# Attention and a squared-ReLU MLP on one core: softmaxes with row maximum, casting loads and a shared set of PSUM banks

## The chip, the cores and the metric

The kernel runs on one core of one Trainium2 chip. The metric is the device time of an execution in microseconds (us), median of the runs shown. The traces come from the hardware profiler. Engines: PE multiplies matrices (PEld loads its weights), DVE works on vectors, ACT evaluates activations, POOL is a slower general engine, SP only issues DMAs here. ACT and POOL can issue DMAs too.

## What is computed

For each of 8 batches and 8 heads, 32 packing queries p attend to 576 keys and values, and the 32 packed rows are then both keys and values for the 576 queries q. The result, laid out as 4608 tokens of 512, goes through an MLP with a squared ReLU. All inputs and outputs are float32.

```python
def sm_attn(qq, kk, vv):
    s = scale * np.matmul(qq, kk.transpose(0, 1, 3, 2))
    s = s - np.max(s, axis=-1, keepdims=True)
    a = np.exp(s)
    a = a / (np.sum(a, axis=-1, keepdims=True) + 1e-09)
    return np.matmul(a, vv)
p_packed = sm_attn(p, k, v)
out = sm_attn(q, p_packed, p_packed)
...
h = x @ w_in
r = np.maximum(h, 0.0)
return ((r * r) @ w_out).astype(np.float32)
```

## The kernel before

Everything on PE is in bfloat16. The work goes batch by batch (b = 0 to 7), the eight heads as two quads (qd = 0, 1) of four heads, whose 4 x 32 packed rows fill 128 partitions or columns. The steps carry names that both texts use:

- **Loads.** SP issues every load of k, q, v (lines 404 and 411) and of the weights (434, 443) as float32 into staging tiles, and also the stores of the output (651, four for each 128 tokens). Only the first load of p comes from ACT. After the load a cast to bfloat16 is made: for batch 0 by ACT, DVE or POOL, for the others on POOL (line 351, or 349 on ACT), the weights on POOL or DVE.
- **Tk, Tq, X.** DVE transposes k (468) and q (462) in 32 x 32 blocks. X spreads the transposed p into a block matrix `pT_bd`, on POOL from batch 1 on.
- **S1.** Scores of p against k, with the 576 keys on the partitions (478, and 492 for the last 64), then an exponential without any maximum (485, 499).
- **PV.** The weights times v, in PSUM already transposed (513), and the denominators by matmuls with a column of ones (517). XT copies the packed rows out of PSUM as `pq_bd` (DVE and ACT, `pq_block`) and `ppT` (`extract`), with the reciprocal `rD` of the denominators.
- **M.** Since the second attention only mixes 32 packed rows per head, w_in is folded into them: M = ppT times w_in, 8 small matmuls for each of 4 chunks of 512 columns (548). It is copied out with the scale rD, one quad on ACT (556) and one mostly on DVE (558).
- **S2 and N.** Scores of q against the packed rows, packed rows on the partitions (578), exponential with scale rD (585), sums over the 32 rows by a matmul with a block matrix of ones (590), then logarithm, exponential of its negative (595, 600) and a multiply on DVE (606) give the weights `a2`.
- **F1.** For 16 blocks of 128 hidden columns: four matmuls of 288 columns (618), ReLU on ACT (626; on DVE, 628, for three blocks of batch 0) and the square on DVE (633) into `gT`, which holds two batches.
- **F2.** For 36 tiles of 128 tokens: 16 matmuls of 512 columns against w_out (642), a copy out of PSUM (349 or 351) and the stores.

PSUM has three pools: `a` of two banks (S1, PV, M), `h` of two double banks (F1, S2, N) and `o` of two banks (F2).

The order of the work on every engine is fixed when the program is made. `Plan` simulates all steps with given durations and lists them by earliest time; streams are listed by priority (attention ahead of F1, F1 ahead of F2), and a step may name other steps that it follows, slots of buffers that it takes, and slots that it frees. Engines then work through their own lists in order. S1 of batch b comes in the plan after F1 of batch b-2.

Of the kernel before, what the change touches and what calls it, by code (L numbers as in the profile page):

```python
# [10 lines left out]
ALU = mybir.AluOpType  # L11
F32 = mybir.dt.float32
BF16 = mybir.dt.bfloat16

P = 128
D = 64
NP = 32
QH = 4
# [19 lines left out]
class Step:  # L38
# [4 lines left out]
    def __init__(self, name, segs, deps=(), take=(), give=(), lag=0.0):  # L43
        self.name, self.deps, self.take, self.give, self.lag = name, list(deps), list(take), list(give), lag
        self.pieces = [[Piece(self, i, k, p) for k, p in enumerate(st)] for i, st in enumerate(segs)]
        self.give_at = [[(p, t or name) for p, j, t in self.give if j == i] for i in range(len(segs))]


class Plan:
# [3 lines left out]
    def __init__(self, slots):  # L53
        self.nslots = slots
        self.streams, self.base = [], {}
        self.fill = 0
# [4 lines left out]
    def forward(self):  # L61
# [4 lines left out]
        held, done, out = {}, {}, []  # L66
        pos = [0] * len(self.streams)
# [3 lines left out]
        def ready(st, t):  # L71
# [7 lines left out]
            for p, n in st.take:  # L79
# [8 lines left out]
                t = max(t, last[p])  # L88
            return t, pred

# [34 lines left out]
        while True:  # L125
            best = None
            for i, (prio, steps) in enumerate(self.streams):
# [7 lines left out]
                if key is None:  # L135
                    key = greedy(pc, t) + 0.003 * prio
                if t < INF and (best is None or key < best[0]):
                    best = (key, pc, t, pred, i)
            for x in pend:
                key = x[0].late  # L140
                if key is None:
                    key = greedy(x[0], x[1]) + 0.003 * (x[2] - 0.5)
# [4 lines left out]
            _, pc, t, pred, src = best  # L147
            b = None
# [11 lines left out]
            if pc.stage == 0:  # L160
                pos[src] += 1
                since[src] = s
                prio = self.streams[src][0]
                for p, k in st.take:
# [15 lines left out]
            for p, taker in st.give_at[i]:  # L180
                x = (fin + lag, tuple((q, lag) for q in ends))
                for j in held.pop((p, taker)):
                    slots[p][j] = x
            if i + 1 < len(st.pieces):
# [8 lines left out]
            s[pos[i]].name for i, (_, s) in enumerate(self.streams) if pos[i] < len(s)]  # L193
        return out, max(p.end for p in out)
# [39 lines left out]
    def first(self, rounds):  # L234
        best = None
        for r in range(rounds + 1):
            out, T = self.forward()
            v = self.score(out, T)
            if best is None or v < best[0]:
                best = (v, T, [(p, p.start, p.end, p.alt) for p in out])  # L240
# [9 lines left out]
    def vary(self, best, seed):  # L250
# [15 lines left out]
        return self.score(out, T), T, [(p, p.start, p.end, p.alt) for p in out]  # L266

    def run(self, rounds=0, seeds=()):
# [4 lines left out]
        self.log = []  # L273
        free = dict(self.base)
# [13 lines left out]
def kernel_impl(tc, q, k, v, p, w_in, w_out, out):  # L288
# [7 lines left out]
    NCB = DMODEL // P  # L296
    NWC = DFF // WCH
    HALF = S // 2
    JH = JT // 2
    TOK = B * S  # L300
    NW = 6
    NT = TOK // P

    with ExitStack() as ctx:
        ctx.enter_context(tc.manual_schedule())
        consts = ctx.enter_context(tc.tile_pool(name="consts", bufs=1))
        stg = ctx.enter_context(tc.tile_pool(name="stg", bufs=4))
        qkv = ctx.enter_context(tc.tile_pool(name="qkv", bufs=4))
        vpool = ctx.enter_context(tc.tile_pool(name="vpool", bufs=1))
# [5 lines left out]
        ps_att = ctx.enter_context(tc.tile_pool(name="ps_att", bufs=2, space=bass.MemoryType.PSUM))  # L315
        ps_h = ctx.enter_context(tc.tile_pool(name="ps_h", bufs=2, space=bass.MemoryType.PSUM))
        ps_o = ctx.enter_context(tc.tile_pool(name="ps_o", bufs=2, space=bass.MemoryType.PSUM))
# [5 lines left out]
        ones_bd = consts.tile([P, P], BF16, name="ones_bd")  # L323
        ones_c = consts.tile([P, 33], BF16, name="ones_c")
        msk = consts.tile([P, 32], BF16, name="msk")
        kT = consts.tile([P, NQD, (GM + 1) * P], F32, name="kT")
        idle_b = consts.tile([P, 256], BF16, name="idle_b")
        v_f = consts.tile([P, H, (GM + 1) * D], F32, name="v_f")
        pT = consts.tile([P, B * NQD, 32], F32, name="pT")
        pT_bd = [consts.tile([P, 896], BF16, name=f"pT_bd{i}") for i in range(2)]  # L330
        pq_bd = [consts.tile([P, 896], BF16, name=f"pq_bd{i}") for i in range(2)]

# [20 lines left out]
        def setup():  # L353
            nc.vector.memset(v_f[:, :, GM * D:], 0.0)
            nc.vector.memset(pT_bd[0][:, :BDW + 2 * P], 0.0)
            nc.vector.memset(ones_c[:, :1], 8.0)
            nc.vector.memset(msk, 0.0)
            nc.vector.memset(msk[:].rearrange("p (x y) -> p x y", y=4)[:, :, :2], 8.0)
# [541 lines left out]
```

## Time and profile before

| | |
|---|---|
| median of 3 runs | 272.71 us (270.44 to 276.31) |
| profiled execution, its span on the core | 272.6 us |
| PE busy | 245.0 us, 1840 matmuls |
| DVE, ACT, POOL busy | 169.6, 167.8, 80.1 us |
| HBM read, written | 37.22 MB, 9.44 MB |
| mean granted PE clock | 0.980 |

The profile has one execution. Its page gives the busy time of the engines and, in 40 slices of the span, the busy share in tenths (9 is 90% or more) of each engine and of the 16 DMA engines. Matmuls are pipelined, so the duration of one is longer than its spacing from the next; the spacing is what a full PE pays. A group of instructions is given by line, engine, operation, output<-inputs, shapes and count, then busy time, mean duration in ns and the idle time before it with its cause. The chain in order of time is followed back from the last instruction, at each step to what released it: start, duration, what.

### The profile page before, as it was taken

The numbers are of one execution on the slowest core, as the hardware profiler recorded it, in microseconds if no ns is written. First come the engines' busy times: TensorE is split into PE (matmuls) and PEld (weight loads), VectorE is DVE, ScalarE is ACT, GpSimd is POOL, SyncE is SP. The second block draws the span as 40 slices with busy tenths as digits, with TensorE's granted clock in tenths as the row PEclk, the third lists the DMA queues.
The fourth block names the chain that finished last, engine by engine and source line by source line (L and its number), as shares of the span: only waits on it lengthen the run. The fifth ranks groups of instructions, "written<-read, shape, count | busy, mean of one in ns | idle before, by whom it ended". The sixth has DMA issues, their size and how long they took to land.

```text
span 272.6 us, 5046 instructions
## 1 busy us (share of the span) xinstructions
PE 245.0 (90%) x1840; PEld 136.5 (50%) x1840; DVE 169.6 (62%) x327; ACT 167.8 (62%) x298; POOL 80.1 (29%) x99
## 2 busy tenths in 40 slices
PE   0558859999998889989999999999999999999993
PEld 0522533555664345745655665566446646644441
DVE  4658997999798498599687648963354504510000
ACT  3547735966786857778659776877657816831110
POOL 5242595592594831443170403000000000000000
PEclk9999995999999979999999999999999999999999
DMA  7999999965949994149328412110211122112222
GB/s 257 321 377 396 383 386 394 358 214 159 319 164 287 364 356 151 42 135 368 95 63 248 182 31 59 41 36 22 62 41 39 39 59 59 40 42 76 77 77 77
DMA packets 26744, 46.99 MB, mean 172 GB/s; under 512 B 5728, under 2 KB 13920, under 8 KB 26720
## 3 DMA queue, kind: packets, MB, share of 16 engines
q1 hardware_dynamic: 26192, 46.55, 51.6%
q8 instruction: 14, 0.23, 0.4%
q10 hardware_dynamic: 528, 0.13, 0.2%
q14 instruction: 10, 0.08, 0.1%
HBM read 37.22 MB, written 9.44 MB: 171 GB/s over the span
## 4 chain that ended last, share of the span: by engine, by line
PE 52%; DMA 18%; DVE 15%; SPq 5%; POOL 3%; issue 3%; ACT 2%; POOLq 0%; DVEq 0%
PE ps_o L642 29%; PE ps_h L618 15%; DVE gT L633 6%; DMA out_dram<-o_sb 5%; DMA w_f<-in_moe_w_in_dram 5%; DMA kq_f<-in_q_dram 5%; DMA v_f<-in_v_dram 4%; PE ps_a L548 3%; SPq L651 3%; DVE kT L468 3%; DVE M L558 2%; SPq L411 2%; PE ps_s L578 2%; ACT o_sb L349 1%; POOL v_b L351 1%
## 5 line engine op out<-in xcount | busy, mean ns | idle before, releaser
L642 PE MATMUL ps_o<-w_out_b,gT 128*128 128x512 bf16 x576 | 150.5, 383 | 0.5 <-DVE gT L633 0.4
L626 ACT ACTIVATE r<-ps_h 128x576 bf16<-128x576 f32 x125 | 79.4, 652 | 24.2 <-PE ps_h L618 18.1
L633 DVE TENSOR_TENSOR gT<-r 128x576 bf16<-128x576 bf16 x128 | 70.5, 573 | 36.5 <-ACT r L626 35.5
L618 PE MATMUL ps_h<-a,M 128*128 128x288 bf16 x512 | 84.1, 294 | 4.4 <-DVE r L628 3.3
L642 PEld LDWEIGHTS <-gT 128*128 128x128 bf16 x576 | 55.2, 98 | 51.6 <-issue 6.0
L618 PEld LDWEIGHTS <-M 128*128 128x128 bf16 x512 | 50.3, 100 | 33.8 <-issue 7.7
L349 ACT COPY o_sb<-ps_o 128x512 f32<-128x512 f32 x27 | 15.8, 585 | 35.0 <-DMA out_dram<-o_sb 23.0
L556 ACT ACTIVATE M<-ps_a,rD 128x512 bf16<-128x512 f32 x36 | 24.2, 689 | 8.6 <-PE ps_a L548 8.5
L351 POOL CAST q_b<-kq_f 128x1152 bf16<-128x1152 f32 (+1 forms) x16 | 19.0, 1203 | 29.3 <-DVE M L558 12.0
L558 DVE TENSOR_SCALAR M<-ps_a,rD 128x512 bf16<-128x512 f32 x28 | 20.7, 746 | 8.8 <-PE ps_a L548 8.6
L351 POOL CAST v_b<-v_f 128x1280 bf16<-128x1280 f32 (+1 forms) x15 | 18.8, 1280 | 21.1 <-PE ps_pp L517 10.2
L462 DVE STREAM_TRANSPOSE qT<-q_b 128x1152 bf16<-128x1152 bf16 x16 | 21.3, 1358 | 4.0 <-POOL q_b L351 3.9
L548 PE MATMUL ps_a<-w_in_b,ppT 64*32 64x512 bf16 x256 | 17.5, 434 | 4.2 <-DVE M L558 2.8
L468 DVE STREAM_TRANSPOSE kT<-k_b 128x320 f32<-128x320 f32 (+1 forms) x32 | 18.9, 686 | 2.8 <-PE ps_a L492 2.3
L351 POOL CAST k_b<-kq_f 128x1152 bf16<-128x1152 f32 (+1 forms) x15 | 18.1, 1210 | 7.6 <-DMA kq_f<-in_k_dram 6.6
L478 PE MATMUL ps_a<-pT_bd,kT 128*128 128x128 bf16 x128 | 9.6, 230 | 9.4 <-DVE pT_bd L351 8.0
L585 ACT ACTIVATE e<-ps_s,rD 128x576 bf16<-128x576 f32 x16 | 11.3, 739 | 9.4 <-PE ps_s L578 6.8
L351 POOL COPY pT_bd<-pT 32x128 bf16<-32x128 bf16 x28 | 10.3, 369 | 21.4 <-PE ps_a L492 15.0
L606 DVE TENSOR_TENSOR a<-e,rs 128x576 bf16<-128x576 bf16 x16 | 14.2, 890 | 0.0
L478 PEld LDWEIGHTS <-kT 128*128 128x128 bf16 x128 | 8.4, 103 | 11.5 <-DVE kT L468 9.1
L578 PE MATMUL ps_s<-qT,pq_bd 128*128 128x288 bf16 x64 | 11.3, 315 | 3.1 <-ACT pq_bd L349 1.8
L548 PEld LDWEIGHTS <-ppT 64*32 64x32 bf16 x256 | 4.3, 90 | 19.2 <-issue 17.1
(53 smaller groups left out, 144.9 us busy)
## 6 DMA issues: line engine op xcount, KB each, us to landing
kq_f<-in_k_dram SPq DMA_DIRECT2D x16, 576.0 KB, 7.5
kq_f<-in_q_dram SPq DMA_DIRECT2D x16, 576.0 KB, 7.0
out_dram<-o_sb SPq DMA_DIRECT2D x144, 64.0 KB, 1.7
v_f<-in_v_dram SPq DMA_DIRECT2D x14, 320.0 KB, 4.6
w_f<-in_moe_w_in_dram SPq DMA_DIRECT2D x8, 512.0 KB, 7.6
w_f<-in_moe_w_out_dram SPq DMA_DIRECT2D x8, 512.0 KB, 9.6
v_f<-in_v_dram SPq DMA_DIRECT2D x14, 256.0 KB, 5.9
v_f<-in_v_dram SPq DMA_DIRECT2D x4, 160.0 KB, 5.8
```

Source lines behind the costliest of these rows:

```text
L349: nc.scalar.copy(dst, src)
L351: eng.tensor_copy(dst, src)
L462: nc.vector.transpose(self.qT[:, qd].rearrange("p dh (j a) -> p j dh a", a=32), self.t.qb[qd][:].rearrange("p (j dh dl) -> p j dh dl", dh= ...
L468: nc.vector.transpose(kT[:, qd, :n * P].rearrange("p (g a jp) -> p jp g a", jp=4, a=32)[:, i:i + 2], self.t.kb[qd][:, J0[i] * D:(J0[i] + 2 ...
L478: nc.tensor.matmul(ps[:, g * P:(g + 1) * P], lhsT=kT[:, qd, g * P:(g + 1) * P].bitcast(BF16).rearrange("p (t two) -> p two t", two=2)[:, d ...
L548: nc.tensor.matmul(pss[qd][o:o + 32, :], lhsT=self.ppT[64 * e:64 * e + 64, qd, pr, :], rhs=w_in_b[64 * e:64 * e + 64, qd * 2 + pr, c * WCH ...
L556: nc.scalar.activation(dst, self.psm[c][e], ACT.Copy, scale=self.rD[:, e:e + 1])
L558: nc.vector.tensor_scalar_mul(dst, self.psm[c][e], self.rD[:, e:e + 1])
L618: nc.tensor.matmul(ps[:, c, :HALF], lhsT=a.M[:, qd, fb * FB:(fb + 1) * FB], rhs=a.a2[:, qd, c * HALF:(c + 1) * HALF], start=(qd == 0), sto ...
L626: nc.scalar.activation(dst, src, ACT.Relu)
L633: eng.tensor_tensor(out=gT[:, fb, o:o + S], in0=r, in1=r, op=ALU.mult)
L642: nc.tensor.matmul(po[t], lhsT=gT[:, fb, n0:n0 + P], rhs=w_out_b[:, fb, :], start=(fb == 0), stop=(fb == NFB - 1))
```

## The change

- **First softmax.** S1 is computed with the packed queries on the partitions and the keys along the row, in a double bank. DVE takes the row maximum from PSUM, ACT applies the exponential with the scaled negative maximum as bias, in two pieces (even and odd groups of keys) with accumulated sums, DVE adds the sums, takes the reciprocal and multiplies. PE transposes the five blocks of 128 keys with an identity, and ACT or DVE copies them out of PSUM. PV loses its denominators, and M its scale.
- **Second softmax.** S2 is turned as well: 128 queries on the partitions, groups of 32 packed rows along the row, the last 64 queries of both quads side by side. DVE takes maximum and difference from PSUM, ACT the exponential, DVE sum, reciprocal and multiply, all over 36 groups of 32. PE transposes the result and ACT or DVE copies it out to `a2`. N, the logarithm and its inverse are gone.
- **Loads.** k, q, v, the weights and the later part of p are loaded by POOL straight into bfloat16 tiles; the DMA casts. There are no cast instructions for them and no staging tiles; 12 tiles for k and q (before: 4 staging, 4 cast), 4 for v, which DVE regroups by one copy a batch (two pieces, also on ACT, in batch 0). SP keeps the stores. X is on DVE. w_out is loaded in part ahead of batch 1 and in between its loads.
- **PSUM.** One set of eight banks; a step names the banks that it may use, and the plan picks. F1, S1 and S2 share (0, 1) and (2, 3), transposes and PV have 4 and 5, F2 has 6 and 7 (its third and fourth tile: 2 and 3). M from batch 1 on does two chunks at a time, in (4, 5) and one of the F1 pairs, with one copy of 1024 columns for each chunk, on ACT alone.
- **Plan.** Regrouping, transposes and X of batch b follow the end of F1 of batch b-2. In batch 0 relu is split between ACT and DVE, and the square may be on ACT.

```diff
-        ps_att = ctx.enter_context(tc.tile_pool(name="ps_att", bufs=2, space=bass.MemoryType.PSUM))
-        ps_h = ctx.enter_context(tc.tile_pool(name="ps_h", bufs=2, space=bass.MemoryType.PSUM))
-        ps_o = ctx.enter_context(tc.tile_pool(name="ps_o", bufs=2, space=bass.MemoryType.PSUM))
+        psum = ctx.enter_context(tc.tile_pool(name="psum", bufs=1, space=bass.MemoryType.PSUM))
...
             def dma_kq(self, name, qd):
                 src = {"k": k, "q": q}[name]
-                f = stg.tile([P, JT * D], F32, name="kq_f", tag="kq")
-                nc.sync.dma_start(f, src[self.b, qd * QH:(qd + 1) * QH].rearrange(
+                t = getattr(self, name)[qd] = qkv.tile([P, JT * D], BF16, name=name + "_b", tag="kqb")
+                nc.gpsimd.dma_start(t, src[self.b, qd * QH:(qd + 1) * QH].rearrange(
                     "h (a j) d -> (h a) (j d)", j=JT))
...
+            def dma_v(self, i, h0, h1):
+                n = GM + 1 if i == 0 else GM
+                if i == 0 and 0 < self.b < NV:
+                    nc.gpsimd.memset(self.v_raw[:, :, GM * D:], 0.0)
+                src = v[self.b, h0:h1].rearrange("h (ap x) d -> ap h (x d)", x=VX)
+                nc.gpsimd.dma_start(self.v_raw[i:P:2, h0:h1, :n * D], src[:, :, i * (GM + 1) * D:(i * (GM + 1) + n) * D])
+            def group(self, h0, h1, eng):
+                cast(eng, self.v[:, :, h0 * D:h1 * D].rearrange("p g (h d) -> p h g d", d=D),
+                     self.v_raw[:, h0:h1].rearrange("p h (g d) -> p h g d", d=D))
...
         def dma_w_in(fq, cp):
-            f = stg.tile([P, 2, WCH], F32, name="w_f", tag="w", bufs=NW)
-            nc.sync.dma_start(f, w_in[cp * 2 * P:(cp + 1) * 2 * P, fq * WCH:(fq + 1) * WCH].rearrange(
-                "(c p) f -> p c f", p=P))
-            w_f[fq, cp] = f
-
+            nc.gpsimd.dma_start(w_in_b[:, 2 * cp:2 * cp + 2, fq * WCH:(fq + 1) * WCH],
+                                w_in[cp * 2 * P:(cp + 1) * 2 * P, fq * WCH:(fq + 1) * WCH].rearrange("(c p) f -> p c f", p=P))
...
+            def s1(self, qd, u):
+                ps = self.ps1[qd] = pair(u)[:, :, :HALF]
+                        nc.tensor.matmul(ps[:, c], lhsT=pT_bd[self.b % 2][:, blk(qd, dh)],
+                                         rhs=kT[:, qd, dh, c * HALF:(c + 1) * HALF], start=(dh == 0), stop=(dh == 1))
-                nc.scalar.activation(self.e1[:, qd], self.ps1[qd], ACT.Exp, scale=0.125)
+            def s1_max(self, qd):
+                nc.vector.tensor_reduce(self.m1[:, qd:qd + 1], self.ps1[qd], axis=AX.XY, op=ALU.max, negate=True)
+                nc.vector.tensor_scalar_mul(self.n1[:, qd:qd + 1], self.m1[:, qd:qd + 1], 0.125)
...
+                e = e1x[:, qd].rearrange("p (g a i2 i) -> p i i2 g a", i=2, i2=2, a=32)
+                for i, n in (0, GM + 1), (1, GM):
+                    x0 = i * (GM + 1)
+                    nc.scalar.activation(e[:, i, :, :n], self.ps1[qd][:, :, x0 * 32:(x0 + n) * 32].rearrange(
+                        "p c (x a) -> p c x a", a=32), ACT.Exp,
+                        bias=self.n1[:, qd:qd + 1], scale=0.125, accum_out=self.d1[:, qd, i:i + 1])
...
+            def s1_norm(self, qd):
+                nc.vector.tensor_tensor(out=self.t1[:, qd:qd + 1], in0=self.d1[:, qd, 0:1], in1=self.d1[:, qd, 1:2], op=ALU.add)
+                nc.vector.reciprocal(self.r1[:, qd:qd + 1], self.t1[:, qd:qd + 1])
+                nc.vector.tensor_scalar_mul(self.e1n[:, qd], e1x[:, qd], self.r1[:, qd:qd + 1])
+            def s1_tr(self, qd, u):
+                ps = self.pst[qd] = bank(u).bitcast(BF16)[:, :(GM + 1) * P]
+                for g in range(GM + 1):
+                    nc.tensor.transpose(ps[:, g * P:(g + 1) * P], self.e1n[:, qd, g * P:(g + 1) * P], ident[:])
+            def s1_out(self, qd, eng):
+                self.tile_of("e1", att, [P, NQD, GM + 1, P], BF16, bufs=1)
+                cast(eng, self.e1[:, qd], self.pst[qd].rearrange("p (g n) -> p g n", n=P))
...
-                for g in range(GM + 1):
-                    nc.tensor.matmul(ps[:, 256 + qd:257 + qd], lhsT=e1(g, 0, P), rhs=ones_c[:, o:o + 1],
...
-                    nc.scalar.activation(dst, self.psm[c][e], ACT.Copy, scale=self.rD[:, e:e + 1])
-                    nc.vector.tensor_scalar_mul(dst, self.psm[c][e], self.rD[:, e:e + 1])
+            def m_out(self, c, eng):
+                cast(eng, self.M[:, :, c * WCH:(c + 1) * WCH], self.psm[c])
...
+            def s2(self, u):
+                self.ps2 = pair(u)
+                for tt in range(4):
+                    for qd in range(NQD):
+                        c0 = (tt % 2) * 2 * P + qd * P
+                        for dh in range(2):
+                            nc.tensor.matmul(self.ps2[:, tt // 2, c0:c0 + P], lhsT=self.qT[:, qd, dh, tt * P:(tt + 1) * P],
+                                             rhs=self.pq[:, blk(qd, dh)], start=(dh == 0), stop=(dh == 1))
+            def s2_rest(self, u):
+                self.ps2r = bank(u)[:, :P]
+                for dh in range(2):
+                    for qd in range(NQD):
+                        nc.tensor.matmul(self.ps2r[64 * qd:64 * qd + 64], lhsT=self.qT[:, qd, dh, 4 * P:S],
+                                         rhs=self.pq[:, blk(qd, dh)], start=(dh == 0), stop=(dh == 1))
...
+            def s2_max(self, x):
+                nc.vector.tensor_reduce(self.m2[:, g0:g1], self.src2(x), axis=AX.X, op=ALU.max)
+            def s2_sub(self, x):
+                nc.vector.tensor_tensor(out=self.d2[:, g0:g1], in0=self.src2(x),
+                                        in1=self.m2[:, g0:g1].unsqueeze(2).to_broadcast([P, g1 - g0, 32]), op=ALU.subtract)
+            def s2_exp(self, x):
+                nc.scalar.activation(self.e2[:, g0:g1], self.d2[:, g0:g1], ACT.Exp, scale=0.125)
+            def s2_sum(self, x):
+                nc.vector.tensor_reduce(self.t2[:, g0:g1], self.e2[:, g0:g1], axis=AX.X, op=ALU.add)
+                nc.vector.reciprocal(self.r2[:, g0:g1], self.t2[:, g0:g1])
+            def s2_mul(self, x, eng):
+                eng.tensor_tensor(out=self.n2[:, g0:g1], in0=self.e2[:, g0:g1],
+                                  in1=self.r2[:, g0:g1].unsqueeze(2).to_broadcast([P, g1 - g0, 32]), op=ALU.mult)
...
+            def s2_tr(self, qd, u):
+                ps = self.pst[qd] = bank(u).bitcast(BF16)[:, :S]
+                for tt in range(4):
+                    g0 = tt * 8 + qd * QH
+                    nc.tensor.transpose(ps[:, tt * P:(tt + 1) * P],
+                                        self.n2[:, g0:g0 + QH].rearrange("p g i -> p (g i)"), ident[:])
+                o = 64 * qd
+                nc.tensor.transpose(ps[:, 4 * P:S], self.n2[o:o + 64, 32:36].rearrange("p g i -> p (g i)"),
+                                    ident[o:o + 64, o:o + 64])
+            def s2_out(self, qd, eng):
...
+        AB = [(4,), (5,)]
+        HB = [(0, 1), (2, 3)]
+        OB = [(6,), (7,)]
+        plan = Plan({"kqb": NKQ, "vb": NV, "r": 4, "osb": 3}, 8)
...
+        def gate(b):
+            return [f"F1.{b - 2}.{GATE}"] if b > 1 else []
...
+                                    [f"XT.{b}"] + [f"LWI.{c}.{i}" for i in range(2)], banks=[(4, 5)], free=[(1, None)]))
+            for c in range(0, NWC, 2):
+                                banks=[(4, 5) + x for x in HB], free=[(1, None)]))
...
-        ld = load_steps(0) + w_in_load() + load_steps(1) + w_out_load()
+        ld = load_kq(0, "k") + [Step("I", [[[("POOL", 0.7, lambda: masks.make_identity(nc, ident[:]))]]])] + load_v(0, 2) + load_kq(0, "q")
+        for fq in range(NWC):
+            ld += load_wi(fq)
+        ld += load_wo(range(0, 4)) + load_kq(1, "k") + load_v(1, 1) + load_wo(range(4, 6)) + load_kq(1, "q") + load_wo(range(6, 8))
+            ld += ([lp] if b == 2 else []) + load_kq(b, "k") + load_v(b, 1) + load_kq(b, "q")
-        for nm in "kvq":
-            plan.stream(5, sum([cast_steps(b, nm, (A, V, Q) if b == 0 else (Q,)) for b in range(B)], []))
-        plan.stream(5.5, w_in_cast((Q, V)) + w_out_cast((Q, V)))
```

## The prediction

> **What bounds the kernel now.** I read the page first, for who is busy when.
>
> ```profile
> PE 245.0 (90%) x1840; PEld 136.5 (50%) x1840; DVE 169.6 (62%) x327; ACT 167.8 (62%) x298; POOL 80.1 (29%) x99
> ...
> PE   0558859999998889989999999999999999999993
> DVE  4658997999798498599687648963354504510000
> POOL 5242595592594831443170403000000000000000
> DMA  7999999965949994149328412110211122112222
> ```
>
> From the middle on PE is full and nothing else is; before that it has holes, while the DMA engines are full up to about 60 us. A busy digit does not tell that PE runs at its peak, so I priced its work by spacings in the full stretch, from the chain in order of time and the timeline.
>
> ```profile
> 67.59 6.68 DMA kq_f<-in_q_dram
> 74.32 1.15 POOL q_b L351
> ...
> 93.21 4.04 DMA v_f<-in_v_dram
> ...
> 100.01 3.84 DMA out_dram<-o_sb
> ...
> 161.84 0.89 PE ps_a L478 x16
> ...
> 174.00 0.98 PE ps_h L618 x8
> ...
> 217.13 8.85 PE ps_o L642 x41
> ```
>
> An F2 matmul takes 8.85/41 = 0.216 us, a 288-column one 0.98/8 = 0.1225, a 128-column one 0.89/16 = 0.0556. The timeline gives 0.34 for the eight matmuls of a weight fold (142.42 to the next start, 142.76) and 0.42 for PV of one quad, 0.12 of it the denominators (191.16 to 191.58). In all: 576 x 0.216 + 512 x 0.1225 + 96 x 0.1225 + 160 x 0.0556 + 32 x 0.34 + 16 x 0.42 = 225.4 us. The span is 272.6, the median 272.71, so I add to the span. Pricing the matmuls that have started by a given time in the same way: 21.5 us are done by 53, 84.5 by 125, all at 268.0. So PE has lost 31.5 us by 53, 9.0 more by 125, 2.1 more by 268.0; 4.6 us of last eviction and store follow. The change can win in the first two only.
>
> The first loss is loading. The table by stage has, after the busy times, clock, DMA share and GB/s:
>
> ```profile
> 20.00:30.00 10.00, 8.54 (x54) 3.31 (x45) 8.48 (x12) 7.43 (x12) 3.63 (x3) 1.00 1.05 386
> 30.00:40.00 10.00, 5.63 (x75) 4.37 (x76) 9.99 (x15) 5.32 (x13) 7.90 (x7) 0.98 1.04 391
> 40.00:50.00 10.00, 9.99 (x64) 3.85 (x62) 8.52 (x17) 6.05 (x10) 6.79 (x6) 0.68 1.05 386
> 50.00:60.00 10.00, 9.51 (x65) 5.42 (x58) 9.99 (x17) 7.51 (x13) 7.34 (x6) 1.00 0.88 290
> 60.00:80.00 20.00, 19.98 (x179) 12.71 (x177) 18.24 (x35) 14.85 (x28) 10.87 (x18) 1.00 0.70 227
> ```
>
> DVE is full from 30 to 60, though its work is small. The groups with shapes apart tell why: the same squaring in two windows, 30 to 60 (POOL busy 22 of 30 us) and 180 to 210 (POOL idle from 180 on).
>
> ```profile
> L633 DVE TENSOR_TENSOR gT<-r 128x576 bf16<-128x576 bf16 x18 | 15.4, 894 | 0.0
> ```
>
> ```profile
> L633 DVE TENSOR_TENSOR gT<-r 128x576 bf16<-128x576 bf16 x17 | 7.8, 457 | 8.2 <-ACT r L626 7.9
> ```
>
> So POOL's casts stretch it. The second loss, 67 to 104, is the chain quoted: loads, POOL casts and output stores that wait for one another, the loads on SP behind the stores.
>
> **The change, part by part.** *PE.* S1 by 64 x 288 columns is 7.8 for 8.9. Out: denominators 16 x 0.12 = 1.9, N sums 32 x 0.1225 = 3.9. In: 160 transposes, 16 of them half as wide, at 0.0556: 8.5. S2 is 160 x 0.0556 = 8.9 for 7.8. Net +2.7: 228.1. No transpose runs in this trace; the ends are that row and the 288-column one, 0.1225 (+10 us); I take the first, the same shape.
>
> *DVE, by nearest rows.* Reading 576 from PSUM is 0.75, 512 is 0.68, so 1024 is 1.21 and 128 about 0.29; 1152 in SBUF, from 0.73 for 576, is 1.33. First softmax: 16 x (max 0.75 + scale 0.1) = 13.6, and 16 x 0.7 = 11.2 for sum, reciprocal (0.17) and multiply (0.4, between 0.25 and the 0.49 of a 640-wide cast). Second, eight times: max 1.5, subtract 1.5, sum and reciprocal 1.5, multiply 1.33: 46.6. Transposes of q and k 32 x 1.358 = 43.5, expanding p (now on DVE) 8 x 4 x 0.316 = 10.1, regrouping v 8 x 1.2 = 9.6 (0.8 to 1.6: 2560 elements, the weight cast has 0.69 for 1024), squares 128 x 0.457 = 58.5, setup 3.2. Sum 196. Gone: M's DVE half (20.7), a's multiply (14.2), casts.
>
> *ACT.* Relu 83.3; exp of S1 in two pieces with bias and sum, 16 x 1.2 = 19.2 (1.0 from 0.39 and 0.59 for 256 and 512; the accumulated sum, 0 to 0.4, is in no row); M as 28 x 1.0 = 28 (0.585 for 512); exp of S2 8 x 1.12 = 9. Sum 140. Ln and inverse (21.3) go. On either engine: S1 and S2 copies 21.6, pq and ppT 21.2, M of batch 0 4.8, outputs 21: 69. Together 405, about 202 each, against 168 and 170 now with POOL's 80.
>
> *Loads.* 66 DMAs leave SP and take POOL, which loses its casts; only outputs (144 issues) stay on SP, so loads no longer wait behind stores. POOL's issue cost is in no row; between SP's 0.44 and POOL's 1.2 for a whole cast, it hides behind the 1.5 us that a 590 KB tile takes at 386 GB/s. A load that waits for one of 12 k/q tiles holds all loads behind it, three batches ahead of their use. The casting rate is in no row: I take the plain one, 386 GB/s, since the bytes read are the same; ends 10% faster (half the bytes written) and half the rate. By the GB/s of the stages, 2.9, 6.3, 10.2, 14.1 and 18.0 MB have moved by 10, 20, 30, 40, 50 us. In the new order the weights w_in are in after 7.86 MB, at 24; half of w_out at 29; k and v of batch 1 at 35; its q after 14.55 MB, at 41; all of w_out at 44. Now batch 1 comes ahead of all w_out, and F2 starts at 42.
>
> *Batch 0.* The max, scale, split exp, norm, transposes and copy put 3.3 us more in the first chain; the casts of k and v (1.1, and the wait to 13.0 for v) go. Then S2 chain: S2 1.5, 5.8 on DVE, transposes 0.6, copy 0.65. F1 starts at 25.5 (24 by w_in, 27.5 if nothing overlaps), now 24.41.
>
> *To batch 1's F1.* q at 41, its transposes 2.7, S2 1, max and subtract 3, exp 1.1, sum and multiply 2.8, transposes and copy 1.3, handovers 1: 54. DVE and ACT have 17.8 (F1's relus and squares) + 29.8 (attention: 405 less relus, squares, outputs and setup, an eighth) + 2.4 (outputs) = 50 us in that stretch; at the 83% that the two reach from 60 to 80 ((18.24 + 14.85)/40) it ends at 25.5 + 30 = 55.5. I take 55. PE has then done two attentions (S1 1.0, transposes 1.1, PV 0.6, S2 1.1, M 1.4, twice: 10.3), F1 of batch 0 (7.8) and four F2 tiles (13.8): 31.9; lost 23.1, now 31.5.
>
> *After that.* F2 of batch 1 can only follow its F1, no backlog yet: 3 (0 to 5). For the rest 4, between 2.1 and 9.0 of now, nearer to the former, as the chain of 67 to 104 loses its casts and its queue. PSUM: the two F1 pairs now also hold S1, S2 and M, 18.2 + 5.1 + 3.4 + 5.4 = 32 us a batch (22 now) of two times 28; F2's own banks, 15.5 us a batch, cover it. The change adds waits on PE's queue in order: its transposes wait for DVE's norm and multiply, with F1 and F2 matmuls behind them, and each late step holds those; that is in the 4. M's pairing moves nothing on PE. The end, 4.6, stays.
>
> Sum: 228.1 + 23.1 + 3 + 4 + 4.6 = 262.8. By the other engines: 405 less 32 done by 25.5 (setup, batch 0's attention), halved, at 83%: 225, so the last square at 250; half of the last four F2 tiles (8) and 4.6 follow: 263. I say 263.
>
> **Two rules weighed.** Transposes first: here 128-column matmuls last 219 ns on average and yet start 56 ns apart. The Trainium skill ("TensorE: Matmul & The Clock Gate", Part 4: PE-mode transpose) puts a transpose at about 275 ns in a kernel, not counted as activity by the clock gate. Read as spacing, 160 of them are 44 us and the sum 298; read as a duration like the row's 219, nothing changes. I hold to the row.
>
> The squares of 894 and 457 ns above are the row for the second. The Trainium skill ("SBUF — State Buffer", Who interferes with whom) lays such stretching to a port that DVE and POOL share, which agrees, and speaks against loads from POOL: DVE copies in a two-port mode lock out descriptor writing. By it the regroupings and norm multiplies of batches 0 and 1 (about 4 us) would come on top: 267. No run here shows it yet.
>
> **Rivals.** *DVE and ACT become the bound (slower).* The time is 25.5 + 186.5/x + 12.6 at a common occupancy x. At 80% (40 to 60 now) it is 271, at 75% 287; slower by 2% from x = 0.775. For it: 202 us each in long chains on queues with a fixed order. Against: 83% was reached with POOL in the way, and 78% from 140 to 160 with PE full.
>
> *Casting transfers are slow.* The first 41 us scale: 263 + 41(f - 1). Within 2% from f = 1.1, slower from 1.37, 283 at 1.5. For it: no row shows such a transfer. Against: neither HBM bytes nor the size of the runs read change.
>
> *Nothing is won.* The new chain eats the earlier w_out, and the holes stay as now: 228.1 + 42.6 + 4.6 = 275.
>
> **How the numbers follow.** A measurement of this kernel tells about 2% from no change (runs 270.4 to 276.3): 267.3 to 278.2. Forecast 0.50 (253 to 267); nothing won or a milder rival (x near 0.8, f of 1.1 to 1.35) 0.23; DVE and ACT bound 0.16, slow transfers 0.11. Faster 0.50, same 0.23, slower 0.27. The low end takes all small terms at their best (20 lost early, no more later: 253). The high end 283 takes f = 1.5 or x near 0.76, leaving out under 2 in 10.
>
> **What would show it.** F1's first matmul at 25 to 26 and F2 by 32; squares near 460 ns throughout; POOL nearly without busy time; 380 GB/s or more to 45 us; PE full from 58 on; DVE near 196 and ACT with it near 400. Wrong if the loads of w_in land after 27, if PE waits for DVE or ACT after 60, or if transposes start more than 60 ns apart.

## The result and the profile after

The changed kernel takes 313.0 us (median of 4 runs, 311.96 to 313.35), beside 272.0 for the kernel before in the same series: ratio 1.154, 95% interval [1.147, 1.162]. The forecast was 263. In every series some executions of the kernel before lie over 1.5% above its fastest; ratios to it, and differences from it in the experiments, leave these out. The profiled execution has a span of 311.5 us at a granted clock of 0.99; its time is 1.7 us more (313.2), a difference that the prediction had put at nothing.

The page of the changed kernel, its busy times and slices:

```profile
PE 249.4 (80%) x1888; PEld 139.8 (45%) x1888; DVE 203.7 (65%) x437; ACT 183.1 (59%) x336; POOL 44.4 (14%) x76
...
PE   0243596799759888999899889988999799998883
...
GB/s 120 199 205 206 206 198 207 208 176 137 222 8 0 109 204 43 47 19 209 103 34 36 51 22 58 11 64 3 69 2 67 36 36 34 34 36 64 53 51 67
```

PE has lost its full second half: 8s stand among the 9s to the very end, where the kernel before had 9s alone, and the digits of no other engine say why. Priced as in the prediction, PE's matmuls come to 227.8 us (forecast 228.1), so the work is as expected; what grew is the idle time. By 55 us PE has lost 39.3 us (forecast 23.1), from there to its last matmul at 306.0 another 38.9 (forecast 7), and 5.5 follow (forecast 4.6). 227.8 + 39.3 + 38.9 + 5.5 is the span.

The dearest group of the page (busy, mean ns of one, then the idle time ahead of it and what ended most of it), the same group on the page of the kernel before, and the list of PE's waits after the change (us, times, longest) name the largest of the new waits:

```profile
L642 PE MATMUL ps_o<-w_out_b,gT 128*128 128x512 bf16 x576 | 150.5, 383 | 0.5 <-DVE gT L633 0.4
```

```profile
L648 PE MATMUL ps<-w_out_b,gT 128*128 128x512 bf16 x576 | 146.8, 380 | 15.9 <-ACT o_sb L387 14.2
```

```profile
PE ps L648 <- ACT o_sb L387: 14.2, 23, 0.7
PE ps L467 <- DVE kT L459: 11.1, 2, 8.5
PE ps L560 <- DVE ppT L389: 6.2, 6, 1.6
PE ps L496 <- DVE e1n L491: 3.5, 3, 3.0
```

The first F2 matmul of a tile waits 0.6 us for ScalarE's copy of the tile before it, 23 times. Before, no such wait was on PE's list, and F2's 576 matmuls had 0.5 us of idle time ahead of them in all. Yet the two tiles lie in different banks: the plan gives 6 and 7 by turns. The third line of the list is the same kind: the second softmax's last piece goes to one of the banks 4 and 5 and waits for the copies of `ppT` out of the other. (The list's second line is mostly the start, 8.5 for the first k.)

In the chain of waits the end of the kernel shows the first wait bare, since there is no F1 left to fill it. Columns are start, length and what:

```profile
277.54 3.25 PE ps L648 x15
280.79 0.02 issue
280.81 0.59 ACT o_sb L387
281.40 0.04 issue
281.44 3.63 PE ps L648 x16
285.07 0.02 issue
285.10 0.59 ACT o_sb L387
285.69 0.04 issue
285.73 3.63 PE ps L648 x16
```

Matmuls, copy, matmuls, copy: 0.65 of every 4.3 us is PE waiting, with a second bank free beside it.

The loads did what was forecast. The table by stage (PE, PEld, DVE, ACT, POOL, clock, DMA share, GB/s):

```profile
20.00:30.00 10.00, 4.20 (x47) 2.66 (x45) 6.75 (x18) 3.24 (x8) 5.67 (x9) 1.00 1.22 206
30.00:40.00 10.00, 5.12 (x37) 2.69 (x37) 5.50 (x12) 3.11 (x7) 5.30 (x8) 1.00 1.24 204
40.00:50.00 10.00, 8.86 (x61) 4.86 (x60) 8.55 (x19) 8.40 (x21) 4.98 (x9) 1.00 1.39 199
50.00:60.00 10.00, 6.60 (x73) 3.84 (x71) 8.42 (x17) 8.12 (x20) 4.15 (x8) 1.00 1.20 208
```

The page counts the bytes written (288 KB for a load of k that was 576 before); a casting load reads twice as many, so 204 is some 408 GB/s read (the prediction took 386). POOL's "busy" is mostly its issuing of these DMAs, 0.55 (k) to 0.71 us (w_out) each. But from 20 to 40 PE, DVE and ACT are all less than 70% busy, and none of PE's waits ends with a load: batch 0 waits for itself. PE's timeline of it (the bracket holds the idle time before and what ended it):

```profile
16.37 0.71 PE L496 MATMUL ps<-ident,e1n 128*128 128x128 bf16 x5 [2.99 <-DVE e1n L491]
17.86 0.69 PE L496 MATMUL ps<-ident,e1n 128*128 128x128 bf16 x5 [0.78 <-ACT e L387]
...
24.20 0.63 PE L532 MATMUL ps<-w_in_b,ppT 64*32 64x512 bf16 x8
26.26 0.63 PE L532 MATMUL ps<-w_in_b,ppT 64*32 64x512 bf16 x8 [1.44 <-DVE M L389]
28.67 0.42 PE L560 MATMUL ps<-pq_bd,qT 128*64 128x128 bf16 x4 [1.78 <-ACT M L387]
31.30 0.62 PE L532 MATMUL ps<-w_in_b,ppT 64*32 64x512 bf16 x8 [2.21 <-DVE d L577]
33.35 0.63 PE L532 MATMUL ps<-w_in_b,ppT 64*32 64x512 bf16 x8 [1.43 <-DVE M L389]
35.41 0.58 PE L602 MATMUL ps<-ident,n 128*128 128x128 bf16 x4 [1.43 <-DVE M L389]
...
37.59 3.05 PE L618 MATMUL ps<-a,M 128*128 128x288 bf16 x12 [0.73 <-ACT a L387]
```

The second quad's transposes, in the other of the banks 4 and 5, start only when the first's copy is done; the two halves of a fold are copied one after the other (1.43 ahead of the next fold, where one copy is 0.6 to 0.7); F1 starts at 37.59 instead of 25.5.

### The profile page after: what moved, and what is told of

It reads as the page before. It is cut to its first block, busy times and chain, and to the rows that moved or that the text cites. A ratio compares the mean times of both kernels' runs of the same rounds, so it can differ in the third digit from the quotient of the medians.

```text
span 311.5 us, 5119 instructions
## 1 busy us (share of the span) xinstructions
PE 249.4 (80%) x1888; PEld 139.8 (45%) x1888; DVE 203.7 (65%) x437; ACT 183.1 (59%) x336; POOL 44.4 (14%) x76
## 3 DMA queue, kind: packets, MB, share of 16 engines
q0 software_dynamic: 18992, 18.55, 37.6%
## 4 chain that ended last, share of the span: by engine, by line
PE 59%; DVE 20%; ACT 11%; DMA 4%; issue 4%; POOL 1%; SPq 0%; ACTq 0%; DVEq 0%; POOLq 0%
PE ps L648 33%; PE ps L618 14%; ACT o_sb L387 5%; PE ps L553 2%; PE ps L467 2%; DMA v_b<-in_v_dram 2%; PE ps L532 2%; DVE pq_bd L389 2%; PE ps L602 2%; DMA out_dram<-o_sb 2%; DVE t L589 2%; DVE gT L640 2%; ACT pq_bd L387 2%; DVE n L595 1%; PE ps L509 1%
## 5 line engine op out<-in xcount | busy, mean ns | idle before, releaser
L648 PE MATMUL ps<-w_out_b,gT 128*128 128x512 bf16 x576 | 146.8, 380 | 15.9 <-ACT o_sb L387 14.2
L630 ACT ACTIVATE r<-ps 128x576 bf16<-128x576 f32 (+1 forms) x131 | 76.6, 617 | 19.5 <-PE ps L618 16.2
L618 PE MATMUL ps<-a,M 128*128 128x288 bf16 x512 | 80.1, 292 | 5.9 <-ACT M L387 2.0
L640 DVE TENSOR_TENSOR gT<-r 128x576 bf16<-128x576 bf16 x119 | 51.9, 454 | 16.1 <-ACT r L630 15.0
L387 ACT COPY o_sb<-ps 128x512 f32<-128x512 f32 x32 | 18.8, 587 | 33.2 <-PE ps L648 33.2
L387 ACT CAST M<-ps 128x1024 bf16<-128x1024 f32 (+1 forms) x32 | 29.3, 958 | 14.2 <-PE ps L532 13.6
L481 ACT ACTIVATE e1x<-ps,n 128x320 bf16<-128x320 f32 (+1 forms) x32 | 25.3, 904 | 17.9 <-DVE n L474 17.9
L459 DVE STREAM_TRANSPOSE kT<-k_b 128x1152 bf16<-128x1152 bf16 x16 | 21.3, 1358 | 1.1 <-DMA k_b<-in_k_dram 1.1
L467 PE MATMUL ps<-kT,pT_bd 128*128 128x288 bf16 x64 | 11.8, 313 | 11.3 <-DVE kT L459 11.1
L387 ACT COPY e<-ps 128x640 bf16<-128x640 bf16 x15 | 10.4, 692 | 12.3 <-PE ps L509 6.3
L589 DVE TENSOR_REDUCE t<-e 128x36 f32<-128x1152 bf16 (+2 forms) x10 | 11.1, 1110 | 7.2 <-ACT e L583 7.2
L572 DVE TENSOR_REDUCE m<-ps 128x4 f32<-128x128 f32 (+2 forms) x17 | 12.2, 719 | 2.1 <-PE ps L553 1.1
L427 POOL DMA_DIRECT2D v_b<-in_v_dram x18 | 12.2, 684 | 5.0 <-DMA k_b<-in_k_dram 1.8
## 6 DMA issues: line engine op xcount, KB each, us to landing
v_b<-in_v_dram POOLq DMA_DIRECT2D x7, 256.0 KB, 10.6
```

What stands on the lines that cost most here:

```text
L387: nc.scalar.copy(dst, src)
L459: nc.vector.transpose(kT[:, qd].rearrange("p dh (j a) -> p j dh a", a=32), self.t.k[qd][:].rearrange("p (j dh dl) -> p j dh dl", dh=2, dl=32))
L467: nc.tensor.matmul(ps[:, c], lhsT=pT_bd[self.b % 2][:, blk(qd, dh)], rhs=kT[:, qd, dh, c * HALF:(c + 1) * HALF], start=(dh == 0), stop=(dh ...
L481: nc.scalar.activation(e[:, i, :, :n], self.ps1[qd][:, :, x0 * 32:(x0 + n) * 32].rearrange("p c (x a) -> p c x a", a=32), ACT.Exp, bias=se ...
L589: nc.vector.tensor_reduce(self.t2[:, g0:g1], self.e2[:, g0:g1], axis=AX.X, op=ALU.add)
L618: nc.tensor.matmul(ps[:, c], lhsT=a.M[:, qd, fb * FB:(fb + 1) * FB], rhs=a.a2[:, qd, c * HALF:(c + 1) * HALF], start=(qd == 0), stop=(qd = ...
```

## The experiments

**Theory A:** in the new PSUM set each tile is two banks wide, and a matmul into one half of a tile is made to wait for a copy that reads the other half. **Theory B** (the prediction's rival): VectorE and ScalarE bound the kernel, and the copy is only the wait that ends last. Four runs tell them apart; the first splits one tile in two:

```diff
-        ps = [psum.tile([P, 2, 512], F32, name=f"ps{i}") for i in range(4)]
+        ps = [psum.tile([P, 2, 512], F32, name=f"ps{i}") for i in range(3)]
+        po_t = {i: psum.tile([P, 512], F32, name=f"po{i}") for i in (6, 7)}
...
         def bank(u, j=0):
+            if u[j] in po_t:
+                return po_t[u[j]][:, :]
             return ps[u[j] // 2][:, u[j] % 2, :]
```

> The changed kernel, with F2's two PSUM banks (6 and 7) as two tiles of one bank instead of the halves of one two-bank tile; every instruction, its order and its engine stay. Theory A (a matmul into one half of a two-bank tile is made to wait for the copy that reads the other half): the 15.9 us that PE stands idle ahead of F2's matmuls go, 14.2 of them released by the output copy on ScalarE, about 0.6 for each tile: 313 falls by 12 to 16, to 297 to 301, and in the last 20 us the copies lie beside the next tile's matmuls. Theory B (VectorE and ScalarE bound the kernel; the copy is only the wait that happens to end last): the idle time moves to other waits and the time stays above 308.

Measured 294.0 us, ratio to the kernel before 1.089 [1.084, 1.094]: 19.0 less than 313.0, more than expected. The wait on the output copy has left PE's list, and the end of its chain reads:

```profile
262.84 0.49 PE ps L621 x4
263.33 20.30 PE po L651 x94
283.63 0.03 ACTq L390
```

94 F2 matmuls in one stretch, the copies beside them. Nothing else was changed, so theory A holds here, and the halves of the tile were all that stood between the two banks: with them apart, copy and matmul run at once.

```diff
-        ps = [psum.tile([P, 2, 512], F32, name=f"ps{i}") for i in range(3)]
-        po_t = {i: ... for i in (6, 7)}
+        ps = [psum.tile([P, 2, 512], F32, name=f"ps{i}") for i in range(2)]
+        po_t = {i: ... for i in (4, 5, 6, 7)}
...
+                self.psm[c] = [bank(u, j), bank(u, j + 1)] if u[j] == 4 else pair(u, j)
```

> As the run before it, and banks 4 and 5 are tiles of their own too (a weight fold that lies in both is copied out in two halves on ScalarE, 0.17 us more each). Theory A: in batch 0 the two transposes' copies, the halves of each fold and the last two copies no longer follow one another (0.8 + 4 x 0.6 + 0.65 = 3.9 us on the way to F1's first matmul, now at 37.6: about 34), and each later batch saves some 0.3 to 0.6: 291 to 296. Theory B: no gain over 308.

Measured 287.9 us (1.066 [1.059, 1.073]), another 6.1 less. F1 starts at 32.68; the wait at 28.67 above (now at 25.07) is 1.17 instead of 1.78, the copies of the transposes no longer follow one another, and the waits for `ppT` are gone.

The same dependence put into the kernel before:

```diff
-        ps_o = ctx.enter_context(tc.tile_pool(name="ps_o", bufs=2, ...
+        ps_o = ctx.enter_context(tc.tile_pool(name="ps_o", bufs=1, ...
...
-                po[t] = ps_o.tile([P, NE], F32, name="ps_o", tag="o")
+                if "all" not in po:
+                    po["all"] = ps_o.tile([P, 2, NE], F32, name="ps_o", tag="o")
+                po[t] = po["all"][:, t % 2, :]
```

> The kernel before, with F2's two output banks as the halves of one two-bank tile; nothing else. Theory A: each of the 36 F2 tiles now waits for the copy of the one before it, 0.6 us and a handover; PE is full from 125 on, so nearly all of it shows: 272 becomes 287 to 294. Theory B (other work of PE fills such a wait, since F1's matmuls and F2's are mixed): 270 to 278.

Measured 291.8 us (1.084 [1.072, 1.096]), some 22 more than the kernel before in the same series (269.4), and PE's list of waits has the new wait at its head and in third place:

```profile
PE ps_o L644 <- ACT o_sb L349: 15.0, 23, 1.0
...
PE ps_o L644 <- DVE o_sb L351: 4.4, 6, 1.4
```

15.0 + 4.4 = 19.4 is most of the loss. The two directions agree: 19 us one way, some 22 the other, from one declaration.

The maxima, taken out of the changed kernel:

```diff
-                nc.vector.tensor_reduce(self.m1[:, qd:qd + 1], self.ps1[qd], axis=AX.XY, op=ALU.max, negate=True)
-                nc.vector.tensor_scalar_mul(self.n1[:, qd:qd + 1], self.m1[:, qd:qd + 1], 0.125)
...
-                        bias=self.n1[:, qd:qd + 1], scale=0.125, accum_out=self.d1[:, qd, i:i + 1])
+                        scale=0.125, accum_out=self.d1[:, qd, i:i + 1])
...
-                nc.scalar.activation(self.e2[:, g0:g1], self.d2[:, g0:g1], ACT.Exp, scale=0.125)
+                nc.scalar.activation(self.e2[:, g0:g1], self.src2(x), ACT.Exp, scale=0.125)
```

> The changed kernel without the two maxima: no row maximum, no scaling of it, no subtraction; both exponentials read PSUM directly, that of the second softmax in two pieces, and the planner lays out the order again. It takes 38 us of VectorE work away and adds about 2 to ScalarE. Theory A (waits for shared PSUM tiles): F1's first matmul comes 4 to 6 us earlier and the steady part stays: 304 to 309. Theory B (VectorE and ScalarE bound it): 38 us of 387 busy, 10% of the time from 25 on: 284 to 292.

Measured 305.9 us (1.135 [1.124, 1.145]), 7 less, as theory A had it; F1 comes at 30.8. VectorE's busy time fell by 34.6 us (203.7 to 169.1; the 38 of the expectation is near the sum of the single durations, which overlap), and that did not buy 25. Since the false waits might have hidden the price, the same edit with the tiles apart:

> The run with four single-bank tiles, without the maxima: no row maximum, no scaling of it, no subtraction, and the planner lays out the order again. Theory (the maxima cost where they lie in a chain that PE waits for, in batch 0 and 1, and nothing where PE is full): 7 less, as with the shared tiles, 280 to 282, most of it before 70 us. Rival (with the false waits gone VectorE and ScalarE bound the kernel): 38 us less of their 387 take 10% off what follows 33 us: 262 to 265.

Measured 277.3 us (1.017 [1.010, 1.024]): 10.6 less, neither 7 nor 24. The two runs are of different series, in which the kernel before itself is 2.5 us apart (means 270.0 and 272.5), so the 10.6 is good to 2 or 3. PE's own account gives the same: what it has lost by a given time, as above, is the time less the price of the matmuls begun.

| kernel | lost by 55 | 55 to 125 | 125 to the last matmul |
|---|---|---|---|
| changed | 39.3 | 15.9 | 23.0 |
| F2's banks apart | 37.5 | 14.0 | 7.4 |
| four banks apart | 35.1 | 12.0 | 5.7 |
| the same without maxima | 30.7 | 8.0 | 3.4 |

(Where matmul records of F2 are missing from a trace, 32 of 576 in the fourth row, they are counted by their weight loads.) Most of what F2's banks cost lies after 125, where PE is full; the maxima cost 4.4 by 55, 4.0 up to 125 and 2.3 after it, 10.7 in all. The first expectation had most of it before 70 us, where it is 4.2 (37.7 to 33.5); by 90 it is 7.1 (44.9 to 37.8). It was wrong in saying that they cost nothing where PE is full. Whether VectorE's time is what costs, or a chain that PE waits for, the next run asks. PE's list with four banks apart has such a wait:

```profile
PE po L535 <- DVE d L585: 5.2, 7, 2.8
```

A weight fold (L535) waits there for the second softmax's subtraction `d`.

> The run with four single-bank tiles, without the second softmax's maximum and subtraction alone (its exponential reads PSUM directly, in two pieces); the first softmax keeps its maximum. Without both it was 277.3, with both 287.9. If the price follows VectorE's time (24 of the 38 us are the second's), 6.7 of the 10.6 go: 281. If it is the chain ahead of the weight folds and F1 that costs (only the second's subtraction holds a bank and stands behind S2), nearly all go: 278. If the first's maximum, at the head of each batch, is what costs: 285 to 287.

Measured 281.7 us (1.030 [1.022, 1.037]): 6.2 of the 10.6 are the second's, by PE's account 6.1 of 10.7. That is nearest to the first expectation: the second has 23.9 of the 35.4 us by which VectorE's busy time falls without both (203.9 to 168.5), and the price is some 0.3 us for each of them (10.6/35.4). It is not shown that VectorE's time as such is the cause. The series differ (the kernel before is at 270.0, 272.5 and 273.0), the second's share changes along the run (3.2 of 4.4 by 55, 1.2 of 4.0 up to 125, 1.7 of 2.3 after it), and the fold's wait for `d` goes as well.

What is left of the late start was tried by the order of batch 0:

```diff
-  [f"Lv.{b}.{qd}.{i}" for i in range(2)], ...
+  [f"Lv.{b}.{qd}.{i}" for i in range(2)] + ["Tk.0.1"], ...
...
-  [[("ACT", 0.61, ... m_half(c, x, A)), ("DVE", 0.68, ... m_half(c, x, V))] for x in QDS]
+  [[("ACT", 0.61, ... m_half(c, x, A))] for x in QDS]
...
-  banks=[(4, 5)], free=[(1, None)]
+  banks=[(4, 5)] + HB, free=[(1, None)]
```

> The run with four single-bank tiles, and in batch 0 alone: the regrouping of v stands behind k's second transpose on VectorE (it waited 2 us for v there), the four weight folds may use any free pair of banks (they had 4 and 5 alone, which the second softmax's last piece and its transposes use too), and ScalarE does all their copies (VectorE has the maxima). Theory (what is left of the late start, F1 at 32.7 where 24.4 was, is the order of batch 0's chain): F1 starts at 28 to 30 and the time falls by 2 to 4, to 284 to 286. Rival (batch 0 is bound by the landing of the loads): F1 stays at 32 and the time at 288.

Measured 286.4 us (1.051 [1.044, 1.058]), F1 as expected:

```profile
28.17 4.24 PE L626 MATMUL ps<-a,M 128*128 128x288 bf16 x16
```

So the loads did not hold F1 at 32.7. But little of those 4.5 us reaches the end: 1.5 in the time, 2.3 in the spans of the two traces. Batch 1's F1 starts only 1.0 earlier (60.2 for 61.2), and by 90 us PE has lost 43.5 where it had lost 44.9. From 40 to 60 VectorE is busy 17.65 of the 20 us: batch 1's softmax and batch 0's relus and squares share it. Around 84, while batch 2's softmax runs, PE waits 2.4 for ScalarE's copy of a fold in one of F1's pairs (2.1 in the run before). That led to:

> The run with the new order in batch 0, and the weight folds of the later batches one chunk at a time in banks 4 and 5 alone, copied out in two halves by ScalarE or VectorE; F1's pairs of banks then serve S1, S2 and F1 only. It adds 28 x 0.17 = 5 us of copying. Theory (a fold that holds one of F1's two pairs, or the pair of S2, holds F1 and S1 behind it: PE waits 2.4 for ScalarE's copy of a fold at 88): 2 to 4 less, 282 to 284. Rival (the copies in wider pieces were worth it, and the pairs were free when needed): 286 to 290.

```diff
-            if b in SOLO:
+            if True:
...
+                                         [[("ACT", 0.61, ... m_half(c, x, A))]
+                                          + ([("DVE", 0.68, ... m_half(c, x, V))] if b else []) for x in QDS]],
...
-            banks=[(4, 5)] + HB, free=[(1, None)]
+            banks=[(4, 5)] + ([] if b else HB), free=[(1, None)]
```

Measured 285.9 us (1.052 [1.044, 1.060]), no difference that can be told from 286.4. The wait of 2.4 has left PE's list, so the folds' use of F1's pairs, less what the narrower copies cost, is worth nothing; whether a gain and that cost cancel is not shown.

The disputed price of a transpose, measured by itself:

```diff
-                for g in range(GM + 1):
+                for g in list(range(GM + 1)) * 2:
                     nc.tensor.transpose(...
...
-                for tt in range(4):
+                for tt in list(range(4)) * 2:
                     g0 = tt * 8 + qd * QH
```

> The run with four single-bank tiles, each of the 160 transposes on TensorE issued twice into the same place. At the 0.056 us between starts of the row that the prediction took, they are 8.5 us more of PE's work; PE has some 6 us of idle time in batch 0 and 1 that can hold a part of those: 294 to 297. At 0.275 each it would be 44 more: 330.

Measured 296.7 us (1.088 [1.080, 1.096]), 8.8 more for 160 more transposes: 0.055 each. In the trace of the changed kernel they start 0.056 apart (median).

Then the loads alone, in the kernel before (v and the weights like k and q; the casts and staging tiles go; 12 tiles for k and q and 4 for v, as in the changed kernel):

```diff
-                f = stg.tile([P, JT * D], F32, name="kq_f", tag="kq")
-                nc.sync.dma_start(f, src[...
+                f = getattr(self, name + "b")[qd] = qkv.tile([P, JT * D], BF16, name=name + "_b", tag="kqb")
+                nc.gpsimd.dma_start(f, src[...
```

> The kernel before with the casting loads alone: k, q, v and both weights come in as bf16 by DMAs that GpSimd issues, in the order of before; GpSimd's casts, the staging tiles and the weights' casts on VectorE go; VectorE regroups v and expands p; softmaxes, PSUM pools and folds stay. Theory (the loads were forecast rightly, and the loss came from the rest of the change): the squares in 30 to 60 fall back to about 457 ns, no load waits behind a store in 67 to 104, and batch 1's F1 comes earlier: 258 to 266. Rival (the casting loads or GpSimd's issue of them are part of the loss): 272 or more.

Measured 267.8 us (0.982 [0.974, 0.990]): faster, but less than expected. PE waits for w_in from 22.5 to 28.0 and F1 starts at 28.5, so:

```diff
-        ld = load_steps(0) + [Step("I", [stage([("POOL", 1.5, setup_pool)])])] + w_in_load()
+        setup_rest()
+        ld = load_steps(0) + w_in_load()
```

(`setup_rest` has the same fills on VectorE.)

> The kernel before with casting loads, and the setting of constants (pq's and p's blocks, the ones) on VectorE ahead of everything instead of on GpSimd between the loads of batch 0 and those of w_in. Theory (w_in's DMAs were issued 2 to 3 us late behind that work: the moved bytes dip to 100 GB/s at 13 to 20, and PE waits for w_in at 22.5 to 28.0): w_in is in by 25.5, F1 starts at 26 instead of 28.5, and the time falls by 2 to 3 to 265 to 266. Rival (the transfers themselves are late, not their issue): 268.

Measured 266.4 us (0.980 [0.972, 0.987]). F1 starts at 26.2, but the two intervals overlap, so the 1.4 us are not told apart. By its median this is the fastest kernel of the study. Squares from 30 to 60, and two stages of it:

```profile
L617 DVE TENSOR_TENSOR gT<-r 128x576 bf16<-128x576 bf16 x22 | 9.1, 447 | 1.1 <-ACT r L610 1.1
```

```profile
40.00:50.00 10.00, 10.00 (x77) 4.95 (x70) 8.13 (x15) 7.37 (x14) 4.64 (x9) 0.83 1.23 205
50.00:60.00 10.00, 10.00 (x66) 6.21 (x64) 9.24 (x19) 7.76 (x14) 5.63 (x10) 1.00 1.22 214
```

447 ns where the kernel before had 894 in this stretch, with GpSimd issuing DMAs the whole time: it was its casts and copies that stretched VectorE, not its presence. From 55 to 125 PE loses 4.2 us, where it lost 9.0. Last, the other order of loads:

> The run beside it, with the order of loads of the changed kernel: half of w_out ahead of batch 1's k and v, a quarter between them and q, a quarter after it. F2 could start at 32 instead of 40.5, where PE had idle time from 28 to 48, but batch 1's k, v and q land 2.6 to 3.9 us later. Theory (PE's holes before 48 can be filled by F2): 2 less than the run beside it, 263. Rival (batch 1's attention is the chain, and its loads later cost as much as is won): 265 to 268.

Measured 268.7 us (0.990 [0.986, 0.994]), 2.4 more than the run beside it, as the rival had it and 0.7 beyond its range. F2 did start at 30.7, and PE was full from 30 to 40; but from 40 to 50 it is busy 8.23 of 10 us and from 60 to 80 16.72 of 20 (10.00 and 18.28 beside it). The hole was moved: batch 1's attention came later and left PE without work then.

## Why the prediction was wrong

**PE's work: right.** 227.8 for 228.1, and the transposes at 0.055 (0.056 between starts) for 0.0556. The Trainium skill's figure ("TensorE: Matmul & The Clock Gate", Part 4: PE-mode transpose, about 275 ns) is no spacing here: 160 more transposes cost 8.8 us and not 44.

**VectorE and ScalarE: nearly right.** VectorE has 203.7 us for 196; with ScalarE 386.8 for 405. ScalarE's split exponential of a quad takes 1.37 us from its start to the next quad's (13.13 to 14.50) for 1.2: each of its two pieces is followed by a read of its sum, recorded as an instruction of 0.26 to 0.28 us. The read lies inside the piece's own time, and the next instruction starts 0.05 after it; how much of the longer time is the sum's, the bias's or the regrouped output's was not separated.

**Loads: right.** Rate as assumed or a little better: w_in is in at 24.9 for 24, half of w_out at 30.0 for 29, batch 1's q at 41.2 for 41. The issue (0.55 to 0.71) is within the bounds and hidden. The 4 us that the Trainium skill ("SBUF — State Buffer", Who interferes with whom) let one fear do not show: VectorE regroups v of batch 0 at 10.4 and of batch 1 at 44.1, and the rate is 205 GB/s from 10 to 20 and 199 from 40 to 50. POOL's issues wait there for earlier loads to land, so a short hold-up of an issue would not be seen. F2, forecast to start by 32, started at 41.6: not for its weights, but 4.0 behind the late F1, as with four banks apart (36.7 behind 32.7). By themselves the loads are worth some 5.3 us (2%, the kernel before at 271.7 against 266.4); the forecast's terms that rest on them, 31.5 to 23.1 by 55 and 11.1 to 7 after it, had claimed 12.5.

**The step that failed.** "PSUM: the two F1 pairs now also hold S1, S2 and M, 18.2 + 5.1 + 3.4 + 5.4 = 32 us a batch (22 now) of two times 28; F2's own banks, 15.5 us a batch, cover it." It priced how long banks are held, and not which instructions the program makes wait for one another. It put the waits of F2 on its own banks at nothing, and they were 14.2 us on PE's list and 19.0 in the time. One line of the change held it, the `ps = [...]` at the head of the first experiment's diff: banks that were tiles of their own in `ps_a` and `ps_o` became halves of `ps[2]` and `ps[3]`. The terms "3 + 4" for everything after 55 are 38.9. With F2's banks apart they are 21.4, with 4 and 5 apart too 17.7, without the maxima as well 11.4 (each the start of the last matmul, less 227.8, less what was lost by 55); in the time the two pairs are worth 19.0 and 6.1, half of the 50 us by which the forecast was off. Of the other half, some 12 are lost by 55 (35.1 for 23.1 with four banks apart) and some 11 after it (17.7 for 7). "The change adds waits on PE's queue in order ... that is in the 4" named waits of the maxima's kind; without the maxima PE loses 6.3 less after 55, more than the whole 4.

**Batch 0** (F1 at 25.5, in fact 37.6). With all four banks apart it is 32.7, with another order in the chain 28.2; some 2.7 remain, within the bound of 27.5 "if nothing overlaps" but for 0.7. Batch 1's F1, forecast for 55, started at 66.8, with four banks apart at 61.2 and with the other order at 60.2. The prediction added the softmaxes' operations to batch 0's chain and left out that the folds' copies (eight halves of 0.6 to 0.7, four of them on VectorE) stand in VectorE's queue between them, and that the folds share banks 4 and 5 with the last piece of S2. The order was the smaller error: 4.5 us of it were worth 1.5 to 2.3 at the end.

**The rivals.** Slower it became, but not as the rival had it: two declarations of tiles took 25 us off without removing one VectorE or ScalarE instruction, and at 313 us the two are busy 62% on average ((203.7 + 183.1)/2/311.5). What the rival has right is a part: by it the maxima's work would have been worth 23 to 26 us with the tiles apart, and it was worth 10.6. Slow transfers: no. Of the signs given for being wrong, "PE waits for DVE or ACT after 60" is what came; its cause was in none of the three rivals.

**Open.** The changed kernel with tiles apart and without maxima (277.3) stays 11 above the kernel before with casting loads (266.4). Some 2.5 of that is PE's extra work; by PE's account 1.7 more is lost by 55 (30.7 for 29.0) and 5.9 more after it (11.4 for 5.5), which was not taken apart. What holds batch 1's F1 near 60 once batch 0's starts at 28 was not tested; the busy VectorE from 40 to 60 is the likely cause, not a shown one.

## What to carry to other kernels

When PSUM is laid out anew, ask of every two banks whether they are one tile: here a write to one half waited for a read of the other, and a bank that is free by count is not free by the program's waits. The Trainium skill ("Perfetto Trace Analysis", Optimizing Tensor Performance, Matmuls) says to rotate matmul groups through the banks so that a copy overlaps the next group; here the banks were rotated and nothing overlapped until they were tiles of their own, 19 us. And price a change of several parts one part at a time: the loads alone were a gain of 2% that the rest buried.

## What the runs showed of the hardware

- A casting load issued by GpSimd moves at the rate of a plain one: some 204 GB/s written, 408 read, with 0.55 to 0.71 us of issue for 256 to 320 KB; but k's lands 8.4 us (median) after its issue, in a queue kept full, so the loads have to be issued well ahead of their use.
- VectorE's squares take 447 ns each from 30 to 60 us while GpSimd issues casting loads, and 894 in the kernel before, where it casts and copies.
- A transpose of 128 x 128 bf16 on TensorE adds 0.055 us to a full queue, the same as a matmul of 128 columns.
- ScalarE's exponential with an accumulated sum is followed by a read of the sum, recorded as an instruction of its own of 0.27 us (32 here, 8.7 us); it overlaps the exponential, so 8.7 us is not its price.
